# Sigmoid attention and GELU feed-forward on one core: six weight loads issued from GpSimd's queue instead of SyncE's

## The chip, the cores and the metric

The kernel runs on one core of one Trainium2 chip. The metric is the device time of one execution in microseconds (us). A core has five engines that run beside each other and wait for one another through semaphores: TensorE (PE; its weight loads are listed apart as PEld), VectorE (DVE), ScalarE (ACT), GpSimd (POOL) and SyncE (SP). SP, ACT and POOL can issue transfers (DMAs). What SP issues runs in the profile's queue q1 (hardware_dynamic), what POOL issues in q0 (software_dynamic). Each engine works through its own instructions in program order.

## The reference

```python
def _attn_ref(q, k, v):                      # q, k, v: 8 x 12 x 448 x 64, float32
    scores = scale * np.matmul(q, k.transpose(0, 1, 3, 2)) - np.log(S)
    attn = 1.0 / (1.0 + np.exp(-scores))
    return np.matmul(attn, v)

def _moe_ref(x, w_in, w_out):                # x: 3584 x 768, w_in: 768 x 2048, w_out: 2048 x 768
    h = x @ w_in
    g = 0.5 * h * (1.0 + erf(h * inv_sqrt2))
    return g @ w_out
```

The attention output, its heads side by side, is the x of the feed-forward.

## The kernel before

The kernel has two stages. Attention runs over 48 pairs of heads in 24 units; each unit makes scores, sigmoids and weighted values, and parks its part of x in SBUF or in the DRAM scratch `scr_x`. The feed-forward then runs in four passes over the batch (`for b in range(NB)`), each pass with `ffn1` (x times w_in, GELU) and `ffn2` (times w_out). Both products are done with seven block products instead of eight (p = 1 to 7), and every float32 operand is split into a high and a low part, so that one product takes three matmuls (`terms`, L579).

The weights come to the kernel as 64-bit words. `Decoder` turns them into float32 while the rest runs, in 28 chunks: 16 of w_in, then 12 of w_out. For each chunk `load` (L127) fetches a raw tile of 1 MB (for w_out) into one of three `raw` buffers, `scale` and `place` (ACT, L141 and L152) make the exponent part `me`, `join` (DVE, L171 and L179) and `round` (DVE, L186) make the words `wd`; `round(i)` then issues `load(i + 3)` (L191), which goes into the raw tile that it has just freed. Two chunks fill one `wd` tile, of which there are two (`bufs=2`). From a full `wd` tile of w_out, `post` (L212) stores five of the seven blocks to the scratch `scr_out` through POOL's queue, and `close` (L220, L221) makes and stores the last two (p = 3 and 7). The `join` of a new tile (L171) writes into the `wd` tile before last, so it waits until all stores from that tile have landed.

`Weights` fetches the decoded blocks back in units of 384 KB (`wst`, L298, on SP's queue; four buffers), ACT copies the high part (L309), DVE subtracts for the low part (L316, which frees the buffer and lets the next `wst` be issued), and PE multiplies with the result `whl`. In the first pass all of this lies between the matmuls of `ffn1`: between most of its 56 block products the code takes some steps of the decoder. The order of the instructions on each engine is the order in which the code writes them.

The names that matter below: raw22 to raw27 are the six loads that `load` issues in the feed-forward (before, the first three at 252.53, 264.88 and 269.62 us); wd16, wd18, wd20, wd22 are `wd` tiles, named by their first chunk; `xl_p` is the low part of a block of x (L621 is the helper `combine`).

Of the kernel before, what the change touches and what calls it, by code (L numbers as in the profile page):

```python
# [22 lines left out]
def tile_sigmoid_attention_gelu_ffn(  # L23
# [10 lines left out]
    nc = tc.nc  # L34
# [84 lines left out]
    class Decoder:  # L119
        def __init__(self):  # L120
            self.raws, self.parts, self.rest, self.out = {}, {}, {}, None
            self.done = self.groups = self.closed = 0
            self.mixing, self.pending, self.open, self.second = [], [], [], None
            self.steps = self.work()
            self.taken = 0

        def load(self, i):  # L127
            if i < len(CHUNKS):
                src = CHUNKS[i][0].bitcast(U16)
                rows, w = src.shape[1], CHUNKS[i][1]  # L130
                raw = sb.tile([P, RAW], U32, tag="raw", name=f"raw{i}", bufs=3)
                dst = raw.bitcast(U16)[:, : 4 * w].rearrange("p (r n) -> p r n", r=rows)
                nc.sync.dma_start(dst[:, :, : 4 * w // rows - 1], src[:, :, 1:])
                self.raws[i] = raw

        def scale(self, i):
# [122 lines left out]
    dec = Decoder()  # L259
# [72 lines left out]
    def x_tile(tag, name):  # L332
        pool, bufs = (sb, 4) if tag == "xs" else (late, 1)
        return pool.tile([P, KC, S], F32R, tag=tag, name=name, bufs=bufs)
# [29 lines left out]
    def attention(at, ps):  # L364
# [163 lines left out]
        for i in range(10):  # L528
            nc.tensor.matmul(warm[:, 0], ready[:, :P], ready, start=True, stop=True)  # L529
        load(0)  # L530
        load_v(0)
        load(1)
        load_v(1)
        load(2)
        for u in range(total):
            for p in range(2):
# [49 lines left out]
    def feed_forward(banks):  # L586
# [281 lines left out]

        seconds = {}
        dec.second = second  # L870
        h2, t4 = (x_tile(f"xt{i}", f"x0_{i}") for i in range(2))
        nc.scalar.copy(h2, x0[1, 0].bitcast(F32))
        nc.scalar.activation(one, one, AF.Gelu)
# [12 lines left out]
    late = ctx.enter_context(tc.tile_pool(name="late", bufs=1))  # L886
    banks = [ctx.enter_context(psum(f"ps_f{n}", (4, 2, 2)[n])) for n in range(3)]
    feed_forward(banks)


# [31 lines left out]
```

## Time and profile before

| | us |
|---|---|
| median of 3 runs | 1015.89 (1015.17 to 1016.56) |
| the profiled execution, whole | 1015.95 |
| its span in the profile | 1013.9 |
| PE busy in the span | 1005.8 (99%) |
| DVE / ACT / POOL busy | 704.5 / 679.4 / 116.1 |
| DMA issued by SP (q1) | 158.53 MB, 51.2% of 16 engines' span |
| DMA issued by POOL (q0) | 41.30 MB, 11.3% |

The span is what the profile covers; the profiled execution is 2.05 us longer than it, and 0.06 us above the median. Attention ends and the feed-forward begins at about 242.7 us, where the first matmul of L584 starts. The clock granted to TensorE was 1.00 of full speed, its level of 2.4 GHz, in every stretch up to 1007.8 us.

### The profile page before, as it was taken

To read this page: it belongs to the slowest core of one execution; us is meant where nothing else is said; L and a number is where in the kernel's file an instruction comes from. 1 tells how busy PE (TensorE), PEld (TensorE's weight loads), DVE (VectorE), ACT (ScalarE), POOL (GpSimd) and SP (SyncE) were. 2 spreads that over 40 slices of the span, in tenths; PEclk is the share of its full clock that TensorE was granted. 3 is DMA by queue.
4 is the path that set the end of the run, shared out by engine and by line. 5 is a ranking of instruction groups with operands and counts; after the bars stand their busy time and mean duration, and the time that the engine had idled before them with its cause. 6 is when DMAs were issued, how large, how long until landed. Compare 5 with 4: busy or idle time off the path is not lost.

```text
span 1013.9 us, 16551 instructions
## 1 busy us (share of the span) xinstructions
PE 1005.8 (99%) x6406; PEld 908.2 (90%) x6406; DVE 704.5 (69%) x822; ACT 679.4 (67%) x935; POOL 116.1 (11%) x186
## 2 busy tenths in 40 slices
PE   9999999999999999999999999999999999999998
PEld 5656666566999999999999999999999999999998
DVE  3677767787788997774378867534887774368873
ACT  5888887788887656467665655766666567665652
POOL 1342223232322210010000000100000000000000
PEclk9999999999999999999999999999999999999999
DMA  9999999997996674564344445634445543334441
GB/s 271 294 352 354 306 334 322 352 337 249 317 334 225 200 245 149 165 205 137 115 130 133 145 141 165 203 124 121 136 113 143 163 153 118 110 109 125 143 141 59
DMA packets 84141, 201.22 MB, mean 198 GB/s; under 512 B 9760, under 2 KB 34336, under 8 KB 84064
## 3 DMA queue, kind: packets, MB, share of 16 engines
q1 hardware_dynamic: 71056, 158.53, 51.2%
q0 software_dynamic: 12704, 41.30, 11.3%
q8 instruction: 50, 0.82, 0.3%
q10 hardware_dynamic: 304, 0.34, 0.1%
q14 instruction: 27, 0.22, 0.1%
HBM read 156.10 MB, written 41.29 MB: 195 GB/s over the span
## 4 chain that ended last, share of the span: by engine, by line
PE 83%; issue 8%; DMA 5%; DVE 2%; POOL 1%; ACT 1%; SPq 0%; POOLq 0%; DVEq 0%; ACTq 0%
PE pf L584 72%; PE pav L470 6%; PE sc L437 4%; DMA scr_x<-x 2%; DMA scr_in<-wd 1%; PE sc_t L454 1%; POOL scr_x L516 1%; DMA scr_out<-wd 1%; DMA wst<-scr_in 1%; DVE wd L171 1%; DVE whl L316 0%; PE warm L529 0%; ACT a L415 0%; DVE xl_p L621 0%; DMA out_dram<-tmp 0%
## 5 line engine op out<-in xcount | busy, mean ns | idle before, releaser
L584 PE MATMUL pf<-op,whl 128*128 128x448 f32 x2016 | 382.0, 352 | 0.0
L584 PEld LDWEIGHTS pf<-op,whl 128*128 128x128 f32 x2016 | 381.0, 189 | 0.3
L584 PE MATMUL pf<-xh_p,whl 128*128 128x448 f32 x1296 | 353.3, 353 | 1.5 <-ACT g L732 1.5
L309 ACT CAST whl<-wst 128x768 fp32r<-128x768 f32 x224 | 186.5, 833 | 212.9 <-PE pf L584 186.5
L316 DVE TENSOR_TENSOR whl<-wst,whl 128x768 fp32r<-128x768 f32 x224 | 213.7, 955 | 145.5 <-ACT whl L309 145.2
L584 PEld LDWEIGHTS pf<-xh_p,whl 128*128 128x128 f32 x1296 | 244.9, 189 | 3.3 <-ACT g L732 1.8
L584 PE MATMUL pf<-xl_p,whl 128*128 128x448 f32 x600 | 211.6, 353 | 1.5 <-DVE xl_p L621 1.5
L415 ACT ACTIVATE a<-sc 128x896 f32<-128x896 f32 x144 | 119.2, 935 | 35.6 <-PE sc L437 35.5
L470 PE MATMUL pav<-a,v 64*64 64x448 f32 x1296 | 133.0, 541 | 0.0
L621 DVE TENSOR_TENSOR op<-g,op 128x896 fp32r<-128x896 f32 x112 | 121.4, 1084 | 0.9 <-ACT op L631 0.9
L584 PEld LDWEIGHTS pf<-xl_p,whl 128*128 128x128 f32 x600 | 113.4, 189 | 1.9 <-DVE xl_p L621 1.8
L470 PEld LDWEIGHTS pav<-a,v 64*64 64x64 f32 x1296 | 55.4, 132 | 61.1 <-issue 33.7
L631 ACT CAST op<-g 128x896 fp32r<-128x896 f32 x112 | 104.8, 936 | 2.6 <-PE pf L584 2.6
L621 DVE TENSOR_TENSOR g<-g,g 128x896 f32<-128x896 f32 x64 | 69.4, 1084 | 0.0
L618 ACT ACTIVATE g<-tmp 128x448 f32<-128x448 f32 x64 | 40.4, 631 | 26.7 <-DVE tmp L621 26.6
L621 DVE TENSOR_TENSOR tmp<-pf,g 128x448 f32<-128x448 f32 x64 | 39.8, 623 | 26.2 <-PE pf L584 25.6
L341 POOL DMA_DIRECT2D x<-scr_x x24 | 18.0, 807 | 325.3 <-ACT g L728 219.3
L437 PE MATMUL sc<-lo,hi 64*128 64x448 f32 x276 | 51.5, 368 | 0.3 <-DVE x L508 0.3
L407 DVE TENSOR_TENSOR lo<-qk,hi 128x896 fp32r<-128x896 f32 x46 | 50.1, 1089 | 1.1
L437 PE MATMUL sc<-hi,lo 64*128 64x448 f32 x276 | 48.9, 349 | 0.0
L437 PE MATMUL sc<-hi 64*128 64x448 f32 x276 | 48.9, 349 | 0.0
L171 DVE SCALAR_TENSOR_TENSOR wd<-raw,me 128x768 uint32<-128x768 uint32 (+1 forms) x28 | 30.0, 1072 | 20.6 <-ACT me L152 11.3
(74 smaller groups left out, 773.1 us busy)
## 6 DMA issues: line engine op xcount, KB each, us to landing
wst<-scr_in SPq DMA_DIRECT2D x112, 384.0 KB, 3.2
wst<-scr_out SPq DMA_DIRECT2D x112, 384.0 KB, 3.1
v<-v_dram SPq DMA_DIRECT2D x48, 256.0 KB, 8.6
raw<-w_in_dram SPq DMA_DIRECT2D x16, 767.8 KB, 7.2
raw<-w_out_dram SPq DMA_DIRECT2D x12, 1023.5 KB, 7.8
qk<-q_dram SPq DMA_DIRECT2D x23, 448.0 KB, 10.9
qk<-k_dram SPq DMA_DIRECT2D x46, 224.0 KB, 11.4
out_dram<-tmp SPq DMA_DIRECT2D x43, 224.0 KB, 2.1
```

What stands on the lines that cost most here:

```text
L171: nc.vector.scalar_tensor_tensor(bits, words, 13, self.parts.pop(i), op0=ALU.logical_shift_right, op1=ALU.bitwise_or,)
L309: nc.scalar.copy(hl[:, 0], t)
L316: nc.vector.tensor_tensor(hl[:, 1], t, hl[:, 0], op=ALU.subtract)
L341: queue.dma_start(dst[:, :, a], src[:, :, a])
L407: nc.vector.tensor_tensor(lo, raw, hi, op=ALU.subtract)
L415: nc.scalar.activation(to, sc, AF.Sigmoid, bias=NEG_LOG_S, scale=SCALE)
L437: nc.tensor.matmul(sc[:, j], ks[rows(j), 1, keys], braid(qs[rows(j), 0]) if braided else qs[rows(j), 0], start=n == 0, stop=n == last,)
L470: nc.tensor.matmul(pav[rows(j), p], vals[u][half, p, j, c], a[p][half, j], start=not swap and c == order[0], stop=c == (order[-1], FULL - ...
L584: nc.tensor.matmul(bank, a, braid(m), **flags)
L618: nc.scalar.activation(straight(dst), unbraid(src), AF.Gelu)
L621: nc.vector.tensor_tensor(out, a, b, op=op)
L631: nc.scalar.copy(op[:, 0], src)
```

## The change

`Decoder` gets an attribute `queue`, SyncE's at first; `load` issues through it. When the feed-forward is set up, the attribute becomes GpSimd's queue. The loads of the attention stage stay where they were.

```diff
@@ class Decoder: __init__
             self.mixing, self.pending, self.open, self.second = [], [], [], None
+            self.queue = nc.sync
             self.steps = self.work()
@@ load
-                nc.sync.dma_start(dst[:, :, : 4 * w // rows - 1], src[:, :, 1:])
+                self.queue.dma_start(dst[:, :, : 4 * w // rows - 1], src[:, :, 1:])
                 self.raws[i] = raw
@@ feed_forward
         dec.second = second
+        dec.queue = nc.gpsimd
```

No instruction is added or taken away, and PE, DVE and ACT keep their order. On POOL, from the stores of wd16 to those of wd18 (`scr_out3` and `scr_out7` are the blocks p = 3 and 7), there stood before:

```order
L221 DMA scr_out3_0_99<-wd16_2733 512x1x128
L221 DMA scr_out7_0_107<-wd16_2733 512x1x128
L212 DMA scr_out2_0_97<-wd18_2973 512x1x128
L212 DMA scr_out4_0_101<-wd18_2973 512x1x128
L212 DMA scr_out1_0_95<-wd18_2973 512x1x128
L212 DMA scr_out5_0_103<-wd18_2973 512x1x128
L212 DMA scr_out6_0_105<-s2_1_3255 512x1x128
L221 DMA scr_out3_0_99<-wd18_2973 512x1x128
L221 DMA scr_out7_0_107<-wd18_2973 512x1x128
```

There stands now, with every line number one higher:

```order
L134 DMA raw22_3192<-w_out_dram 128x2x2047
L222 DMA scr_out3_0_99<-wd16_2733 512x1x128
L222 DMA scr_out7_0_107<-wd16_2733 512x1x128
L213 DMA scr_out2_0_97<-wd18_2973 512x1x128
L213 DMA scr_out4_0_101<-wd18_2973 512x1x128
L213 DMA scr_out1_0_95<-wd18_2973 512x1x128
L213 DMA scr_out5_0_103<-wd18_2973 512x1x128
L213 DMA scr_out6_0_105<-s2_1_3255 512x1x128
L134 DMA raw23_3283<-w_out_dram 128x2x2047
L134 DMA raw24_3343<-w_out_dram 128x2x2047
L222 DMA scr_out3_0_99<-wd18_2973 512x1x128
L222 DMA scr_out7_0_107<-wd18_2973 512x1x128
```

One raw load now stands ahead of the last two stores of wd16, two ahead of the last two of wd18. On SP, at the same place of the program, the loads of the decoded weights (`wst`) had raw loads among them:

```order
L133 DMA raw22_3192<-w_out_dram 128x2x2047
L298 DMA wst8_3201<-scr_in8_75 128x768
L298 DMA wst9_3230<-scr_in9_76 128x768
L298 DMA wst10_3269<-scr_in10_77 128x768
L133 DMA raw23_3283<-w_out_dram 128x2x2047
L298 DMA wst11_3300<-scr_in11_78 128x768
L298 DMA wst12_3329<-scr_in12_79 128x768
L133 DMA raw24_3343<-w_out_dram 128x2x2047
L298 DMA wst13_3366<-scr_in13_80 128x768
```

Now they follow one another:

```order
L299 DMA wst8_3201<-scr_in8_75 128x768
L299 DMA wst9_3230<-scr_in9_76 128x768
L299 DMA wst10_3269<-scr_in10_77 128x768
L299 DMA wst11_3300<-scr_in11_78 128x768
L299 DMA wst12_3329<-scr_in12_79 128x768
L299 DMA wst13_3366<-scr_in13_80 128x768
```

The `wst` loads have lost the raw loads that stood ahead of them in their queue.

## Rows read from the trace of the kernel before

**Rows 1.** Busy time by stretch: stretch, length, busy us (count) per engine, clock, DMA.

```profile
240.00:283.00 43.00, 39.75 (x207) 36.65 (x204) 32.77 (x36) 34.15 (x51) 13.70 (x20) 1.00 0.86 305
283.00:1007.80 724.80, 724.80 (x3831) 723.80 (x3831) 504.11 (x542) 452.46 (x655) 34.55 (x47) 1.00 0.50 152
```

**Rows 2.** PE in order of time: start, length, what [idle before, releaser].

```profile
275.73 0.46 PE L584 MATMUL pf<-xh_p,whl 128*128 128x448 f32 x1 [1.47 <-ACT g L732]
282.79 0.46 PE L584 MATMUL pf<-xl_p,whl 128*128 128x448 f32 x1 [1.50 <-DVE xl_p L621]
```

**Rows 3.** PE's weight loads in order of time, at the seventh weight unit.

```profile
263.78 0.19 PEld L584 LDWEIGHTS pf<-xh_p,whl 128*128 128x128 f32 x1 [0.16 <-DVE whl L316]
```

**Rows 4.** DVE in order of time, around its two waits at L171.

```profile
260.89 1.23 DVE L171 SCALAR_TENSOR_TENSOR wd<-raw,me 128x1024 uint32<-128x1024 uint32 x1 [2.64 <-DMA scr_out<-wd]
...
262.75 0.97 DVE L316 TENSOR_TENSOR whl<-wst,whl 128x768 fp32r<-128x768 f32 x1
...
275.25 0.95 DVE L316 TENSOR_TENSOR whl<-wst,whl 128x768 fp32r<-128x768 f32 x1
279.31 1.22 DVE L171 SCALAR_TENSOR_TENSOR wd<-raw,me 128x1024 uint32<-128x1024 uint32 x1 [3.11 <-issue]
...
281.18 1.56 DVE L621 TENSOR_TENSOR xl_p<-x,xh_p 128x1344 fp32r<-128x1344 f32 x1
```

**Rows 5.** The chain of work that ended last: start, length, what.

```profile
270.49 7.48 DMA scr_out<-wd
```

**Rows 6.** ACT in order of time, ahead of PE's wait at 275.73.

```profile
273.51 0.83 ACT L309 CAST whl<-wst 128x768 fp32r<-128x768 f32 x1 [1.27 <-DMA wst<-scr_in]
```

**Rows 7.** SP's issues in order of time; a length spans all issues of its row.

```profile
252.53 0.38 SPq L133 DMA_DIRECT2D raw<-w_out_dram  x1
254.61 9.46 SPq L298 DMA_DIRECT2D wst<-scr_in  x3
264.88 0.38 SPq L133 DMA_DIRECT2D raw<-w_out_dram  x1
265.75 3.08 SPq L298 DMA_DIRECT2D wst<-scr_in  x2
269.62 0.38 SPq L133 DMA_DIRECT2D raw<-w_out_dram  x1
...
326.37 52.62 SPq L298 DMA_DIRECT2D wst<-scr_out  x18
```

**Rows 8.** POOL's issues in order of time.

```profile
253.40 1.46 POOL L221 DMA_DIRECT2D scr_out<-wd  x2 [7.18 <-DVE wd L220]
...
270.49 1.45 POOL L221 DMA_DIRECT2D scr_out<-wd  x2 [10.92 <-DVE wd L220]
...
440.34 1.49 POOL L341 DMA_DIRECT2D x<-scr_x  x2 [80.63 <-ACT g L728]
```

**Rows 9.** Issues near 252.6, 254.2, 271.3 and 441.2: KB each, us to landing.

```profile
raw<-w_out_dram SPq DMA_DIRECT2D x1, 1023.5 KB, 5.9
...
scr_out<-wd POOLq DMA_DIRECT2D x1, 256.0 KB, 6.7
...
scr_out<-wd POOLq DMA_DIRECT2D x1, 256.0 KB, 8.1
...
x<-scr_x POOLq DMA_DIRECT2D x1, 336.0 KB, 4.1
```

**Rows 10.** DMA queues from 253 to 257.4 us: packets, MB, share of 16 engines.

```profile
q1 hardware_dynamic: 228, 0.93, 76.9%
```

**Rows 11.** DMA in all and by queue, from 257.4 to 259.4 us.

```profile
DMA packets 242, 0.79 MB, mean 393 GB/s; under 512 B 37, under 2 KB 37, under 8 KB 242
...
q0 software_dynamic: 145, 0.51, 63.4%
q1 hardware_dynamic: 97, 0.28, 37.0%
```

**Rows 12.** Waits from 283 to 345 us: us in total, times, longest.

```profile
DVE wd L171 <- ACT me L152: 3.5, 2, 2.6
```

## The prediction

> **What bounds the kernel now.** I read the busy time by stretch first. From 283 us to 1007.8 us PE works for 724.80 of 724.80 us, so nothing can be won there, and whatever delays PE before it goes to the end undiminished. From 240 to 283 us, where the decoder of w_out and the first pass of the feed-forward share all engines, PE works for 39.75 of 43 us, and the transfers take 0.86 of the DMA engines at 305 GB/s [rows 1]. The six moved loads lie in and just behind this stretch, so the question is what they do to PE's waits in it. PE in order of time shows two: 1.47 us ended by ACT, and 1.50 us ended by DVE's xl_p [rows 2]. Its weight loads show a third place, of 0.16 us only, ended by DVE's L316: here DVE is just in time [rows 3].
>
> Next I follow each back to what ends it. Two lead to the same cause. DVE stands still at L171 until stores from the tile that it wants to overwrite have landed: 2.64 us up to 260.89, and 3.11 us up to 279.31. Right behind the first comes the L316 (262.75) for which PE waited 0.16 us, right behind the second the xl_p (281.18) for which it waited 1.50 us [rows 4]. The second idle time is put down to "issue", but the chain has a scr_out store, issued at 270.49, just ahead of it [rows 5]; its partner, the second of the two, is issued some 0.7 us later and lands 8.1 us after that, at about 279.2 [rows 8, 9]. So the stores of p = 3 and 7 set PE's time at both places. The third wait, at 275.73, has another cause: ACT's queue stood for 1.27 us at L309 for a wst load [rows 6], which SP had issued at 265.75, right behind raw23 [rows 7].
>
> **The change part by part.** It moves six loads of 1023.5 KB. SP saves six issues; its wst loads wait for DVE's L316, not for the raw loads' own issue, so I cost that at nothing. POOL gets six issues; one takes about 0.7 us (1.46 for two [rows 8]). raw22 would go out at 252.53, 0.9 us before the store at 253.40; raw24 at 269.62, 0.9 us before the store at 270.49 [rows 7, 8]: POOL is free again in time. raw25 to raw27 wait on DVE ahead of stores that nobody reads before the scr_out loads begin at 326.37 [rows 7], some 25 us behind the last of them; and from 283 to 345 us DVE's L171 waits for ACT, not for stores [rows 12]. Their cover is that distance. So three loads count: raw22 for the first join, raw23 and raw24 for the second.
>
> Term A, the first join. The two stores now stand behind raw22 in one queue. Would they not have waited before? They did: from 253 to 257.4 us SP's queue moved 0.93 MB, 228 packets, and POOL's queue has no row at all [rows 10], though the store was issued at 253.40. Standing behind the raw load is therefore no new wait; what counts is how fast a raw load from GpSimd is, and what slips in. No raw load from POOL is in this stage of the trace. The nearest row is the pair of x loads at 440.34: 672 KB in 0.7 + 4.1 = 4.8 us [rows 8, 9]. Another 351.5 KB (0.36 MB) at 393 GB/s [rows 11] take 0.9 us, which makes 5.7 us, against 5.9 us for raw22 from SP [rows 9]. By this the raw load is 0.2 us faster. The bounds: if it ran at 393 GB/s from its first packet, the 0.93 MB that took 4.4 us would take 2.4, a gain of 2.0 us; if it were as slow as on SP and began one POOL issue later, a loss of 0.7 us. I take -0.2, as the pair is the nearest row. What slips in: the wst loads of 254.61 and the one after it are no longer behind raw22 in their queue, so both can be served before the stores; each is 0.39 MB, 1.0 us at 393 GB/s. Before, SP's queue took 0.28 MB beside the stores from 257.4 to 259.4 us, 0.7 us [rows 11]. So 0 to 1.3 us are added; I take the middle, +0.65, as nothing in the trace chooses. A = -0.2 + 0.65 = +0.45 (from -2.0 to +2.0). PE waits at this place already [rows 3], so a positive A passes to it in full.
>
> One rule of the Trainium skill speaks against the change here, and it bears on this middle. The page "DMA: Bandwidth & Descriptors", section "Queues, rings and completion order", says that an engine goes round between the queues for which it has work and drains a whole packet of descriptors, about 9 to 17, before it turns to the next. The trace agrees where a raw load alone moved for 4.4 us while a store was waiting [rows 10]. By it a wst load would take its turn between the raw load and each store, the +1.3 end, and A would be +1.1.
>
> Term B, PE's wait at 275.73. The wst load of 265.75 no longer has raw23 ahead of it, so ACT's 1.27 us [rows 6] should go and PE's 1.47 us become 0.2. This gives PE 1.27 us that it cannot keep: what is late next is the xl_p, whose time the stores of the second join set.
>
> Term C, the second join. Everything on DVE from 260.89 to the end of L316 at 276.2 moves by A, as DVE has no idle time there beyond its 3.11 us [rows 4], and the stores of 270.49 are issued A later. Ahead of them in their queue are now raw23 and raw24, each 0.2 us faster by the estimate above: -0.4. The wst loads that SP issues at 265.75 and behind it share the engines with them before and after alike: 0, or +1.0 for one more that slips in. So the join moves by 0.45 - 0.4 = +0.05, about nothing. Its ends are -6.0 (three raw loads at the fast end), of which PE can keep no more than its waits, 0.16 + 1.27 + 1.50 = 2.9 us; and 2.0 + 1.4 + 1.0 = +4.4 us.
>
> The sum is what PE's last wait moves by: +0.05 us on 1015.95 us for the profiled execution, 1016.0. The median is 0.06 lower, so 1015.9 to the tenth; between unequal ends (2.9 down, 4.4 up) I lean a little up, and say 1016.1.
>
> **The rivals.** No change that a measurement can tell means within 0.2%, 2.03 us.
>
> Slower: the stores land late. If a raw load from POOL is no faster than on SP (0 in place of -0.2) and both wst loads slip in at the first join (+1.3) and one at the second (+1.0), DVE's second wait ends 2.3 us later: 1015.89 + 2.3 = 1018.2. It decides from 2.03 us on. For it speaks that each join stands two instructions ahead of what PE waits for, with no slack [rows 3, 4]; against it that the engines move the same bytes either way. The rule of the page named above gives the +1.3 and the +1.0, and so this case.
>
> Faster: raw loads from POOL come near 393 GB/s, all stores land early, and PE loses all three waits: 1015.89 - 2.9 = 1013.0. For it speaks that q0 and q1 together reached 393 GB/s where SP's raw load alone did not [rows 10, 11]; against it that the pair of x loads was no faster than a raw load, and that some of ACT's work stays ahead of PE. It decides only if 2.03 of the 2.9 us go.
>
> Hidden anyway: both queues share the DMA engines, the same bytes go through in the same time, and the order does not matter; then 1015.9. This lies inside my forecast and cannot be told from it by the time, only by PE's waits.
>
> **How the numbers follow.** The forecast, no measurable change, with the hidden case in it: 0.68, its own range 1014.0 to 1017.9. Slower: 0.21. Faster: 0.11. The same three numbers are the chances. For the range, 8 in 10: below 1014.2 I leave about 0.09, most of the faster case; above 1018.4 about 0.10, the slower case's upper half, in which the raw loads are at the slow end of term A. The time is that of the likeliest, 1016.1.
>
> **What would show it.** In the profile of the changed kernel: 1. q0 carries 6.3 MB more and q1 as much less. 2. ACT no longer waits for a wst load at 273.5, and PE's wait of 1.47 us is near 0.2. 3. DVE's L171 starts near 261.3 (A = +0.45); at 262.2 or later the slipping-in is what counts, at 259 or earlier POOL's raw load is fast. 4. The second L171 starts near 279.4, and PE's last wait, ended by xl_p, is then some 2.3 us (1.50 + 1.27 - A + 0.05): the sum of PE's waits stays about 3.2 us. 5. A raw load takes 5.7 us and more to land. 6. No wait of PE behind 283 us. I am wrong if PE waits later than that, if the joins move by over 2 us, or if POOL holds the stores back because an issue of a raw load takes it far longer than 0.7 us.

## The result and the profile after

The changed kernel takes 1022.65 us in the median of 6 runs (1021.71 to 1023.86), the kernel before 1016.27 us in 6 runs beside them; the ratio is 1.0061 (95% interval 1.0051 to 1.0072). So the change is slower by 6.4 us, where 1016.1 us and a range up to 1018.4 were forecast.

The profiled execution took 1022.73 us, its span is 1020.6 us, 6.7 us more than before. I read it in the order of the prediction. First the busy time by stretch (stretch, length, busy us and count of PE, PEld, DVE, ACT, POOL, then clock, DMA share, GB/s), to be set beside [rows 1]:

```profile
240.00:287.00 47.00, 40.00 (x208) 36.48 (x204) 32.48 (x36) 36.09 (x52) 16.22 (x23) 0.98 0.82 285
287.00:290.00 3.00, 2.94 (x8) 2.69 (x9) 3.00 (x5) 0.00 (x0) 0.42 (x1) 0.50 0.37 126
290.00:295.00 5.00, 5.00 (x22) 4.78 (x21) 4.97 (x6) 2.40 (x5) 1.81 (x3) 0.77 0.78 201
295.00:360.00 65.00, 65.00 (x345) 64.59 (x344) 57.35 (x71) 48.11 (x71) 16.43 (x23) 1.00 0.75 240
```

PE is still always busy after 287 us. But in the 3 us behind it the granted clock is 0.50, its level of 1.2 GHz, and PE does 8 matmuls there; the 65 us at 1.00 hold 345, which is 16 in 3 us. PE in order of time (start, length, what [idle before, releaser]), beside [rows 2], shows what stood ahead of that:

```profile
249.16 1.78 PE L585 MATMUL pf<-x,whl 128*128 128x448 f32 x8 [0.60 <-DVE x L622]
...
265.46 0.46 PE L585 MATMUL pf<-xh_p,whl 128*128 128x448 f32 x1 [0.90 <-DVE whl L317]
...
287.06 0.74 PE L585 MATMUL pf<-xl_p,whl 128*128 128x448 f32 x1 [5.47 <-DVE xl_p L622]
```

The ACT wait of 1.47 us is gone from PE. ACT's cast of the wst load, beside [rows 6], starts without a wait, and the weight loads, beside [rows 3], have 0.43 us there and 1.25 us at the first join:

```profile
273.81 0.81 ACT L310 CAST whl<-wst 128x768 fp32r<-128x768 f32 x1
```

```profile
265.45 0.19 PEld L585 LDWEIGHTS pf<-xh_p,whl 128*128 128x128 f32 x1 [1.25 <-DVE whl L317]
276.02 0.19 PEld L585 LDWEIGHTS pf<-xh_p,whl 128*128 128x128 f32 x1 [0.43 <-ACT g L733]
```

The wait for xl_p has grown from 1.50 to 5.47 us, and a matmul behind it lasts 0.74 us where the same one lasted 0.46 [rows 2]. The 6.7 us are these two things: PE's waits were 0.28 (at 248.57, not among the rows) + 1.47 + 1.50 = 3.25 us and are now 0.60 + 0.90 + 5.47 = 6.97, which is 3.72 more; and PE's busy time rose from 1005.8 to 1008.8 us, 3.0 more, with the same 6406 instructions. Of these 3.0 us, 2.57 lie behind the wait for xl_p: from the matmul that ends it to the end, PE is busy for 729.88 us, in the kernel before for 727.31.

DVE in order of time shows both joins late, beside [rows 4]; the third row is the end of the rounding that sets raw24's buffer free:

```profile
262.58 1.23 DVE L172 SCALAR_TENSOR_TENSOR wd<-raw,me 128x1024 uint32<-128x1024 uint32 x1 [3.75 <-DMA scr_out<-wd]
...
270.05 1.22 DVE L187 CUSTOM_DVE_ANT_0 wd<-raw,wd 128x2048 uint16<-128x2048 uint16 x1
...
283.58 1.23 DVE L172 SCALAR_TENSOR_TENSOR wd<-raw,me 128x1024 uint32<-128x1024 uint32 x1 [5.70 <-issue]
...
285.45 1.55 DVE L622 TENSOR_TENSOR xl_p<-x,xh_p 128x1344 fp32r<-128x1344 f32 x1
```

The first join begins 1.69 us later than before (262.58 against 260.89), the second 4.27 us (283.58 against 279.31), which includes the 1.69. POOL's issues, beside [rows 8], show why they do:

```profile
253.71 0.72 POOL L134 DMA_DIRECT2D raw<-w_out_dram  x1 [6.90 <-DVE wd L221]
254.42 1.53 POOL L222 DMA_DIRECT2D scr_out<-wd  x2
...
271.85 0.73 POOL L134 DMA_DIRECT2D raw<-w_out_dram  x1 [4.01 <-ACT g L619]
272.57 1.49 POOL L222 DMA_DIRECT2D scr_out<-wd  x2
```

DVE's rounding ended at 270.05 + 1.22 = 271.27, and POOL issued raw24 0.58 us later. Before, the same rounding ended at 269.59 (268.37 1.22 in the kernel before's trace) and SP issued at 269.62, 0.03 us later [rows 7]. The stores then went out right behind the raw load, 272.57. How long the loads and stores took to land (KB each, us), beside [rows 9], for the issues at 253.7, 271.8 and 272.5 us, and the median of the two stores near 273.2 (its row counts two):

```profile
raw<-w_out_dram POOLq DMA_DIRECT2D x1, 1023.5 KB, 6.3
...
raw<-w_out_dram POOLq DMA_DIRECT2D x1, 1023.5 KB, 9.1
...
scr_out<-wd POOLq DMA_DIRECT2D x1, 256.0 KB, 9.7
...
scr_out<-wd POOLq DMA_DIRECT2D x2, 256.0 KB, 9.9
```

raw24 lands at 271.85 + 9.1 = 281.0, the stores behind it from 282.3 on; before, the first store of this pair took 7.48 us [rows 5]. So the delay of the second join has three parts: the rounding ends 1.68 us later (carried over from the first join), raw24's issue on POOL holds the first store back by another 0.40 us (2.08 in all, 272.57 against 270.49), and the store takes 2.2 us longer to land.

The queues show where the 2.2 us come from. In the kernel before, the stores issued at 270.49 stood still at first as well; from 272.3 to 274.4 us only q1 has a row (packets, MB, share of 16 engines):

```profile
q1 hardware_dynamic: 190, 0.63, 97.5%
```

The next 3 us, from 274.4 to 277.4, show the difference. First the kernel before (all packets; then by queue as above):

```profile
DMA packets 319, 1.16 MB, mean 386 GB/s; under 512 B 26, under 2 KB 26, under 8 KB 319
...
q1 hardware_dynamic: 198, 0.73, 64.9%
q0 software_dynamic: 121, 0.43, 35.3%
```

And the changed kernel:

```profile
DMA packets 79, 0.65 MB, mean 216 GB/s; under 512 B 0, under 2 KB 0, under 8 KB 79
...
q0 software_dynamic: 79, 0.65, 82.4%
```

Before, the stores ran in q0 beside q1's transfers, at 386 GB/s together; raw24, issued at 269.62 and 9.2 us under way, was among these. Now raw24 and the stores stand in one queue. The 79 packets have 8.2 KB on average, where those of q0 before, the stores', had 3.6 KB; raw22, running alone on POOL's queue, has about 8 KB too (129 packets with 1.04 MB, see below). So they are raw24's: it runs alone at 216 GB/s, and the stores wait for it. The totals of the page show that the six loads went over as announced, 6.29 MB from q1 to q0:

```profile
q1 hardware_dynamic: 69424, 152.24, 48.7%
q0 software_dynamic: 13568, 47.59, 13.4%
```

### The profile page after: what moved, and what is told of

It is laid out like the page before. It is cut to its first block, busy times and chain, and to the rows that moved or that the text cites. A ratio compares the mean times of both kernels' runs of the same rounds, so it can differ in the third digit from the quotient of the medians.

```text
span 1020.6 us, 16553 instructions
## 1 busy us (share of the span) xinstructions
PE 1008.8 (99%) x6406; PEld 911.5 (89%) x6406; DVE 704.9 (69%) x822; ACT 679.4 (67%) x935; POOL 120.6 (12%) x192
## 4 chain that ended last, share of the span: by engine, by line
PE 94%; DMA 2%; DVE 2%; issue 1%; ACT 1%; POOL 0%; SPq 0%; DVEq 0%; POOLq 0%; ACTq 0%
PE pf L585 72%; PE pav L471 12%; PE sc L438 8%; PE sc_t L455 2%; DMA scr_out<-wd 1%; DMA wst<-scr_in 1%; DVE wd L172 0%; ACT a L416 0%; PE warm L530 0%; DVE whl L317 0%; DVE wd L187 0%; POOL scr_out L222 0%; DMA out_dram<-tmp 0%; DVE x L622 0%; DVE xl_p L622 0%
## 5 line engine op out<-in xcount | busy, mean ns | idle before, releaser
L172 DVE SCALAR_TENSOR_TENSOR wd<-raw,me 128x768 uint32<-128x768 uint32 (+1 forms) x28 | 30.2, 1077 | 24.1 <-ACT me L153 12.8
```

The source lines that it names most:

```text
L172: nc.vector.scalar_tensor_tensor(bits, words, 13, self.parts.pop(i), op0=ALU.logical_shift_right, op1=ALU.bitwise_or,)
```

## The experiments

My theory after this: the cost is the order in the queue. Stores on which a join waits now stand behind a raw load, and POOL issues that load 0.6 us late and takes 0.7 us for it. A wait of PE near 5 us then costs another 2.5 to 3 us, as the clock falls behind it. The rivals: the first join carries it all; a raw load issued by POOL is costly wherever it stands; the 3 us of PE's busy time are not due to its wait. The kernel before ran beside each group (medians 1016.42, 1016.42 and 1016.30 us in 26, 29 and 29 runs).

**raw22 alone on GpSimd.**

```diff
-                nc.sync.dma_start(dst[:, :, : 4 * w // rows - 1], src[:, :, 1:])
+                queue = nc.gpsimd if i in (22,) else nc.sync
+                queue.dma_start(dst[:, :, : 4 * w // rows - 1], src[:, :, 1:])
```

> Only raw22 goes out on GpSimd, the other five stay on SyncE. Theory (order in the queue: the two stores of a join now start behind a raw load of their own queue, about 0.6 us of lag and 0.7 us of issue on GpSimd included): the first join, DVE's store wait, moves from 260.9 to about 262.5, the second from 279.3 to about 280.5, since its stores are only issued later and raw24 is not in their queue; PE's last wait grows from 1.5 to about 2.6 us, its clock stays at 1.00, and the time is 1017.4 us. Rival 1 (the whole loss comes from the first join, what follows only carries it on): 1020 us or more. Rival 2 (it comes from the second join alone): 1016.3.

1017.88 us, ratio 1.0019 (1.0005 to 1.0033). PE in order of time:

```profile
264.91 0.46 PE L585 MATMUL pf<-xh_p,whl 128*128 128x448 f32 x1 [1.05 <-DVE whl L317]
...
277.62 0.46 PE L585 MATMUL pf<-xh_p,whl 128*128 128x448 f32 x1 [2.23 <-ACT g L733]
...
283.61 0.46 PE L585 MATMUL pf<-xl_p,whl 128*128 128x448 f32 x1 [0.43 <-DVE xl_p L622]
```

The median is 1.5 us above the kernel before (1.0 was expected), and rival 1 (1020 or more) falls. The profile shows less than that: the first join begins at 262.04, 1.15 us later than before, PE's last wait ends 0.82 us later, and the waits sum to 3.71 us against 3.25. The delay appears in the waits for whl and for ACT, and xl_p's wait shrinks to 0.43 instead of growing to 2.6. The rest of the 1.5 us is not placed.

**raw23 and raw24** (the same edit with `i in (23, 24)`).

> Only raw23 and raw24 go out on GpSimd. Theory: the first join stays at 260.9; at the second the two stores run behind raw24 instead of beside it and take some 10 us instead of 8, so that xl_p is 2.6 us later, near 283.8; PE's wait for ACT (1.47 us) goes and its last wait becomes about 5.3 us. If the clock falls as it did in the changed kernel behind its wait of 5.5 us, the time is 1016.3 + 2.6 + 3.0 = 1021.9 us, if it does not, 1018.9. Rival (the first join is what counts): 1016.3.

1021.37 us, ratio 1.0058 (1.0037 to 1.0080): the branch in which the clock falls. PE's last wait, and the stretch that begins with it (columns as above):

```profile
285.01 0.74 PE L585 MATMUL pf<-xl_p,whl 128*128 128x448 f32 x1 [4.76 <-DVE xl_p L622]
```

```profile
285.00:288.00 3.00, 2.99 (x8) 2.73 (x9) 3.00 (x4) 0.00 (x0) 0.15 (x1) 0.50 0.41 109
```

The wait is 0.5 us shorter than expected, and again 8 matmuls take 3 us. The 1.5 us of raw22 alone and the 5.0 of these two add up to about the 6.4 us of all six.

**raw24 alone** (`i in (24,)`).

> Only raw24 goes out on GpSimd, right ahead of the two stores of wd18. Theory (the stores run behind raw24 instead of beside it): nearly all of the 5.0 us that raw23 and raw24 cost together, 1020.5 to 1021.5 us; the second join ends near 281.5 and PE's waits for ACT and for xl_p are 5 us together, or the wait for ACT takes over part of it. Since the clock fell behind waits of 4.8 and 5.5 us, the time is some 2.5 us lower (1018.5) if ACT's wait of 1.5 us splits the idle time in two. Rival (the two loads share the cost, or raw23 carries it): 1018 or less with no fall of the clock, and raw23 alone 1018 or more.

1020.87 us, ratio 1.0048 (1.0033 to 1.0064). So this one load, right ahead of the two stores, costs some 4.5 of the 6.4 us. It issues at 269.95, 0.3 us later than before [rows 7]; it, the first store and the pair of issues behind it took to land:

```profile
raw<-w_out_dram POOLq DMA_DIRECT2D x1, 1023.5 KB, 10.1
...
scr_out<-wd POOLq DMA_DIRECT2D x1, 256.0 KB, 10.4
...
scr_out<-wd POOLq DMA_DIRECT2D x2, 256.0 KB, 10.7
```

The first store, issued at 270.66, took 10.4 us in place of 7.48 [rows 5]: 3 us for standing behind raw24 in its queue, where before raw24 was in the other. ACT's wait does split PE's idle time, as I had allowed for, but the clock falls all the same (0.67 from 285 to 288 us), so the branch of 1018.5 was wrong:

```profile
275.24 0.46 PE L585 MATMUL pf<-xh_p,whl 128*128 128x448 f32 x1 [0.78 <-ACT g L733]
...
285.93 0.72 PE L585 MATMUL pf<-xl_p,whl 128*128 128x448 f32 x1 [5.12 <-DVE xl_p L622]
```

**raw23 alone** (`i in (23,)`).

> Only raw23 goes out on GpSimd, some 3 us ahead of the stores of wd18; raw24 runs beside these on SyncE's queue as before. Theory: the wst load is rid of raw23, so PE's wait of 1.47 us for ACT goes, what it gains is waited for at xl_p instead, and the join comes as in the kernel before: 1016.4 us (1015.5 to 1017). Rival (raw23 in the stores' queue is what delays them): 1018 us or more.

1017.00 us, ratio 1.0018 (1.0002 to 1.0033). The ACT wait is gone; these are all of PE's waits from 240 to 290 us (us in total, times, longest):

```profile
PE pf L585 <- DVE xl_p L622: 1.5, 1, 1.5
PE pf L585 <- DVE x L622: 0.6, 1, 0.6
```

2.1 us in all against 3.25 before. The time alone does not rule out the rival (1018 or more), as the interval reaches 1.0033 and three of the twelve runs took over 1020 us. What speaks against it is DVE's wait at the second join, 2.29 us against 3.11 [rows 4], so that raw23 did not delay the stores:

```profile
280.32 1.23 DVE L172 SCALAR_TENSOR_TENSOR wd<-raw,me 128x1024 uint32<-128x1024 uint32 x1 [2.29 <-issue]
```

The profile itself is not shorter than before (span 1015.0 us), as its feed-forward begins at 244.85 us, 2.1 us later than before and ahead of all that the edit touches. The control below has such a start without any edit.

**The wait filled with work.** All six loads on GpSimd, and ahead of the block for which PE waits 5.47 us:

```diff
+                if (b, p, j) == (0, 4, 0):
+                    for _ in range(24):
+                        nc.tensor.matmul(
+                            ph, none, one_s, start=False, stop=False, skip_group_check=True
+                        )
```

> All six loads on GpSimd as in the changed kernel; PE gets 24 more matmuls (128x448, zero weights, adding zero to the sum) ahead of the block for which it waits 5.5 us, 24 x 0.19 = 4.5 us of work in that wait. Theory (the clock fell because PE stood still): the wait becomes about 1 us, xl_p comes as late as before, the clock stays at 1.00 behind it, and the time falls by the 3.0 us that PE's busy time had grown, 1022.65 - 3.0 = 1019.7 us. Rival (the clock fell for another reason, or the 3 us are not the clock): 1022.6 us.

1019.62 us, ratio 1.0033 (1.0022 to 1.0043): 3.03 us less than the changed kernel by the medians, 2.8 by the ratios to the kernel before beside each. PE in order of time:

```profile
280.80 4.77 PE L726 MATMUL pf<-const-float32-1.0,const-float32-0.0 128*128 128x448 f32 x24
...
286.23 0.46 PE L585 MATMUL pf<-xl_p,whl 128*128 128x448 f32 x1 [0.47 <-DVE xl_p L625]
```

xl_p comes nearly as late as in the changed kernel (0.5 us earlier, counted from the start of the feed-forward), PE does 24 matmuls that nobody needs, and the kernel is faster: the matmul behind the wait lasts 0.46 us again, the clock is 1.00 from 287 to 300 us. PE's work from that matmul to the end (stretch, length, busy us and count, first column PE), in the kernel before, the changed one and this one:

```profile
282.79:1014.00 731.21, 727.31 (x3842) 725.97 (x3842) 504.71 (x543) 454.07 (x658) 34.55 (x47) 1.00 0.50 152
287.06:1021.00 733.94, 729.88 (x3842) 728.06 (x3842) 504.85 (x543) 452.01 (x656) 36.87 (x50) 1.00 0.50 151
286.23:1018.00 731.77, 727.31 (x3842) 725.90 (x3842) 504.40 (x543) 451.84 (x656) 36.90 (x50) 1.00 0.50 152
```

The same 3842 matmuls take 727.31 us where the clock stays at 1.00 and 729.88 where it fell. So the clock falls because PE stands still, and that costs 2.6 us in this profile (2.5 with raw23 and raw24 moved, 2.0 with raw24, counted in the same way). That the medians differ by the expected 3.0 is partly chance, since some of it is xl_p coming earlier. The Trainium skill says on its page "TensorE: Matmul & The Clock Gate", section "Part 1: The HAM clock gate (the "warmup" mystery)", that "the default state is throttled, and activity releases the throttle". This run agrees with it: 1.00 behind the filled wait, 0.50 behind the empty one.

**Ten matmuls in the wait** (`range(10)`).

> All six on GpSimd, with 10 added matmuls instead of 24 ahead of the block for which PE waits: PE stands for 5.5 - 1.9 = 3.6 us. The clock fell behind waits of 4.8, 5.1 and 5.5 us and not behind 2.2 us. If a wait of 3.6 us leaves it at 1.00, the time is 1019.7 us, if not, some 1022.3.

1023.80 us (1021.30 to 1026.13), ratio 1.0070 (1.0047 to 1.0093): the second branch. In the profile the remaining wait of 3.84 us still lets the clock fall, to 0.53 from 287 to 290 us and 0.60 from 290 to 295. It does not always: the run of 1021.30 us had a clock of 1.00 over its whole length, the other five 0.996 to 0.998.

```profile
281.72 2.08 PE L726 MATMUL pf<-const-float32-1.0,const-float32-0.0 128*128 128x448 f32 x10
...
287.82 0.74 PE L585 MATMUL pf<-xl_p,whl 128*128 128x448 f32 x1 [3.84 <-DVE xl_p L625]
```

**raw22, raw24 and raw25 behind the stores**, all six on GpSimd.

```diff
-            self.load(i + 3)
+            if i + 3 in (22, 24, 25):
+                self.due.append(i + 3)
+            else:
+                self.load(i + 3)
@@ at the end of close, behind its two stores
+            while self.due:
+                self.load(self.due.pop(0))
```

> All six loads on GpSimd, but raw22, raw24 and raw25 are issued behind the two stores of the join instead of ahead of them; raw23 stays where it was. Theory (order in the queue): the stores go at once, the first join ends at about 258.5 or earlier instead of 260.9 (before) and 262.6 (changed), the second at about 276, PE's waits shrink from 3.2 us to under 1 us, and the time is 1013.5 to 1015 us: faster than both kernels. Rival 1 (a raw load issued by GpSimd is costly by itself, wherever it stands): 1019 us or more. Rival 2 (raw tiles now land too late for DVE's join of them): a new wait of DVE for a raw load, 1016 us or more.

1014.70 us, ratio 0.9984 (0.9970 to 0.9998), faster than both kernels. The stores of wd16 and the raw22 behind them took to land:

```profile
scr_out<-wd POOLq DMA_DIRECT2D x1, 256.0 KB, 2.7
...
scr_out<-wd POOLq DMA_DIRECT2D x1, 256.0 KB, 4.4
...
raw<-w_out_dram POOLq DMA_DIRECT2D x1, 1023.5 KB, 9.5
```

The second of the two stores, which decides, took 4.4 us in place of 6.7 [rows 9]: DVE has no store wait at the first join any more. The loads are as large as before and on the same queue, so a raw load issued by POOL need not cost time by being there: rival 1 falls, and so does rival 2, since raw22's 9.5 us are in time for its join. Two details came out otherwise: the second join begins at 279.71, not 276, behind a wait for stores of 2.58 us (the feed-forward begins 2.0 us later in this profile), and PE's waits sum to 1.63 us, not under 1.

**raw23 also behind** (`if i + 3 in (22, 23, 24, 25)`).

> As the version that loads raw22, raw24 and raw25 behind the stores of the join, with raw23 also behind them. Theory: the second join comes some 3 us earlier still, near 276.5 on the same base, but PE did not wait for xl_p there any more, and its other waits are for ACT and for x; so the time stays at 1014.7 (1014.0 to 1015.2). Rival (raw23 and raw24 now land too late for their own joins): DVE waits for a raw load near 288, 1016 us or more.

1014.23 us, ratio 0.9979 (0.9970 to 0.9988). At the second join DVE runs through without a wait, and PE's only wait up to 283 us is for ACT. DVE, then PE:

```profile
273.96 1.22 DVE L173 SCALAR_TENSOR_TENSOR wd<-raw,me 128x1024 uint32<-128x1024 uint32 x1
...
275.85 1.53 DVE L628 TENSOR_TENSOR xl_p<-x,xh_p 128x1344 fp32r<-128x1344 f32 x1
```

```profile
274.44 0.46 PE L591 MATMUL pf<-xh_p,whl 128*128 128x448 f32 x1 [0.32 <-ACT g L739]
```

DVE now waits at 282.34 for stores at another line (2.95 us), which PE does not feel. New are two waits for `tmp`, 0.6 us together.

**raw25 to raw27 alone** (`i in (25, 26, 27)`), and once more in another group.

> Only raw25, raw26 and raw27 go out on GpSimd, behind the last wait of PE. Theory: no PE wait answers to them, 1016.4 us as before (within 0.7). Rival (they delay the stores that the second pass reads back, or DVE): 1017.5 us or more.

> raw25 to raw27 on GpSimd once more. Theory (their loads stand ahead of the stores of the fourth join, DVE waits 1 us longer there, and PE waits some 0.5 us for tmp): 1017.0 us, and in a profile whose feed-forward starts where it did before, 0.5 us more of waits. Rival (the 1.6 us are a property of these loads): 1018 us again, with PE's waits larger than before by 1.5 us.

1018.01 us, ratio 1.0015 (1.0005 to 1.0024), and 1019.26 us, ratio 1.0023 (1.0010 to 1.0036): the theory's "as before" fell, and so did the 1017.0 of the second; both times the rival's figure came out. PE's waits behind 300 us in the second of the two:

```profile
322.61 0.46 PE L585 MATMUL pf<-xh_p,whl 128*128 128x448 f32 x1 [0.77 <-DVE tmp L622]
...
343.65 0.46 PE L585 MATMUL pf<-xh_p,whl 128*128 128x448 f32 x1 [0.35 <-DVE tmp L622]
```

They follow a wait of DVE's L172 at 317.73 of 4.11 us; before, its longest between 283 and 345 us was 2.6 us [rows 12]. With them, PE's waits of the feed-forward sum to 3.6 us here against 3.25 before: that is 0.3 us of the 2.3 that the ratio gives, so the rival's mechanism, 1.5 us more of PE's waits, is not there either. In both profiles the feed-forward begins over 2 us late (245.16 and 244.86). Where the rest of the medians' loss is from stays open. In the changed kernel no wait of PE answers to these three loads, since all of its waits lie ahead of 288 us.

**A control**, the kernel before with a comment added.

> Nothing differs from the kernel before but a comment. raw25 to raw27 alone cost 1.6 us, of which the profile shows some 0.5 us in PE's waits, and in that profile the feed-forward begins 2.4 us later, ahead of all that the edit touches. If such a shift comes from the program and not from the edit, the control shows one as well, up to 1.5 us either way; if not, it runs at 1016.4 within 0.5.

1016.97 us (1014.48 to 1022.49), ratio 1.0003 (0.9989 to 1.0018). Its profile has the late start too, 244.36 us, behind this wait in the attention, near 40 us (us in total, times, longest):

```profile
PE sc L438 <- ACT a L416: 1.3, 1, 1.3
```

So a single profile can lie 2 us off for a reason ahead of the edit, and the waits of the feed-forward have to be compared from its own start. These waits sum to 2.7 us here against 3.25 in the kernel before, with no edit between them: differences of some 0.5 us in them, such as that of raw22 alone, can be chance. The control's median lies 0.7 us above that of the same kernel beside it, for nothing.

**raw22 to raw24 behind the stores, raw25 to raw27 on SyncE** (`if i + 3 in (22, 23, 24)`, these three on GpSimd).

> raw22, raw23 and raw24 on GpSimd behind the stores of the joins, raw25 to raw27 on SyncE as before. Theory: PE's waits of the feed-forward's first 60 us go as with all six behind, and the 0.6 us of waits for tmp near 318 and 339 us go too: 1013.6 us, the fastest. Rival (raw25's place matters for the third join): 1015 us or more.

1016.34 us, ratio 0.9999 (0.9985 to 1.0013): my expectation fell, and the rival's figure (1015 or more) came out; whether raw25's place is the reason, no run shows. The waits for `tmp` did not go with raw25 to raw27 back on SyncE; they are 1.1 us (0.6 with all six behind). I take it that PE comes to that place earlier than in the kernel before and meets a later join there. That accounts for 0.5 us of the 2.1 us between the two versions (all of PE's waits in the feed-forward for 0.9); the rest I can't place.

## Why the prediction was wrong

*What bounds the kernel* was right: the changed kernel lost time by PE's waits ahead of 288 us and by what they did to the clock. (A wait of 0.28 us for x, at 248.57, was overlooked.)

*Term B* was right: the ACT wait of 1.47 us went, and PE could not keep it.

*Term A* (+0.45, bounds -2.0 to +2.0): the size was within its bounds, but by other parts than those of the sum. The join came 1.69 us later, but 0.59 of it lies ahead of raw22: the rounding before it ended at 253.10 instead of 252.51. The rest is 1.1 us. I had put +0.65 on wst loads that slip in and -0.2 on a faster raw load. Nothing slipped in: from 253 to 259.4 us only q0 has a row, with raw22 (packets, MB, share):

```profile
q0 software_dynamic: 129, 1.04, 65.0%
```

And raw22 took 6.3 us in place of 5.9, 0.4 more instead of 0.2 less. What I left out is that POOL issues raw22 about 0.6 us after the rounding, where SP took 0.03. I costed the issue as "POOL is free again in time", which counted its 0.7 us alone. Nor did the delay pass to PE "in full": [rows 3] is a wait of the weight loads, PE itself had none there, and it got one of 0.90 us.

*Term C* is the step that failed. "Ahead of them in their queue are now raw23 and raw24, each 0.2 us faster by the estimate above: -0.4" treats the stores as if they had to follow raw24 before as well. That nearly holds for raw22 [rows 10], and I carried it over to the second join without a look at the queues there. Up to 274.4 us the stores stood still there too, but from 274.4 to 277.4 they ran beside q1's transfers, raw24 among them, at 386 GB/s in all. In one queue they run behind raw24, and it alone moves 216 GB/s. The join came 4.27 us later in place of 0.05. Of this 1.69 are carried over from the first join, where +0.45 stood; the other 2.6 stand against the -0.4. raw24 by itself moved to GpSimd makes the first store take 10.4 us instead of 7.5, and the kernel some 4.5 us slower. That 4.27 lies within the upper end of +4.4 us is luck: that end was made of slow raw loads and of wst loads that slip in. My range stopped at 1018.4, 2 us short of that end.

*The price of a wait* was missing altogether. I counted a microsecond of PE's wait as a microsecond of time. Behind the wait of 5.47 us the clock was 0.50, and PE's work from there on took 2.6 us more; the run with the filled wait gives these 2.6 us back. A sum with the right join would still have missed them. [rows 2] had waits of 1.5 us only, so no row of the kernel before showed it. A range that reached to a long wait should have had this on its upper side.

*The rivals.* "The stores land late" was the right one, with the right place (two instructions ahead of PE's wait, no slack), and 0.21 was too little for it. Its mechanism, wst loads that slip in, was not the one: in the two stretches where raw22 and most of raw24 run, from 253 to 259.4 and from 274.4 to 277.4 us, q1 has no row. "Faster" and "hidden anyway" failed: the order in the queue matters, by 3 us of landing for the store behind raw24. Of the Trainium skill's page "DMA: Bandwidth & Descriptors" I weighed the rule on turns between queues (section "Queues, rings and completion order"). The turns that I took from it for the wst loads did not come in these stretches. What decided was plainer: work of two queues can overlap on the engines, as the row at 386 GB/s shows, and work of one queue, by the row at 216 GB/s, did not.

*What would show it*: items 1 (6.29 MB), 2 and 5 (6.3 to 9.1 us) came true, item 3 came out beyond its 262.2 mark (262.58), but not for the reason that this mark was to show, item 4 failed (283.58 for 279.4, 5.47 us for 2.3), and of item 6 it holds that no wait begins behind 283 us, while the last one reaches to 287.06 and the work behind it took longer.

## What to carry to other kernels

Before moving a load to another queue, look at what stands behind it there, and whether that ran beside the load before: here one 1 MB load ahead of two stores cost some 4.5 of the 6.4 us, and all six on the same queue, the first four of them behind the stores, made the kernel 2.1 us faster than it was. Price a growing wait of PE above its length, as the clock may fall behind it (2 to 3 us here); and compare waits from the start of their own stage, since another stage can shift a single profile by 2 us.

## What the hardware showed that I had not expected

A raw load alone on the engines moved 216 GB/s (79 packets with 0.65 MB in 3 us, 82.4% of the engines' time), two queues together 386 GB/s. POOL issued a load 0.58 us after the work that it waited for, SP 0.03 us after it. In the profiles the clock fell behind PE waits of 3.84, 4.76, 5.12 and 5.47 us, to 0.50 in the worst stretch, which cost 2.0 to 3.2 us of PE's time, and stayed at 1.00 behind waits of 1.5 and 2.23 us.
